# Gated attention and two expert layers on one core: the second unit's first layer, the search marks, the small experts and the last scatters change places

## The chip, the cores and the metric

One core of a Trainium2 chip runs the whole kernel in one launch. The metric is the device time of one execution in microseconds (us), as the median of several runs. A profiled execution of the same program gives the trace; its span is the time from the first to the last instruction on the core. Engines are named as the profile names them: PE (matrix multiplies, with PEld for its weight loads), DVE (VectorE), ACT (ScalarE), POOL (GpSimd) and SP (the queue that issues most DMAs).

## What is computed

```python
def _attn_ref(q, k, v, alpha):                      # 4 x 8 heads, 768 steps, 48 wide
    for t in range(S):
        state = alpha[:, :, t, :, None] * state + np.einsum('bhd,bhe->bhde', k[:, :, t], v[:, :, t])
        y[:, :, t] = np.einsum('bhd,bhde->bhe', q[:, :, t], state)

def _moe_ref(x, w1, w2, w3, w_out):                 # 3072 tokens of 384, hidden 768
    return np.maximum(np.maximum(x @ w1, x @ w2), x @ w3) @ w_out

def _moe2_ref(x, w_gate, w_output_gate, w1, w2):    # 8 experts, hidden 1024
    e_idx = np.argmax(x @ w_gate, axis=1)           # one expert for each token
    for e in range(E):
        mask = e_idx == e
        h = np.maximum(x[mask] @ w1[e], 0.0)
        out[mask] = gate_w[mask, None] * eom[mask, e, None] * (h @ w2[e])
```

## The kernel before, in words

**Stages.** Up to about 456 us of the profile the kernel runs the recurrence and the dense layer, block by block (8 blocks of 384 tokens), and writes the 3072 result rows to a table in DRAM (`x2d`). The rest, which the change touches, is the expert layer. Each product is computed with operands split into a high and a low part, so one product is three matmuls.

**Units.** An expert's tokens are cut into units of up to 256 tokens, two result tiles of 128. A unit is *kind 0* (two tiles, plain), *kind 2* (two tiles and a third of up to 64 tokens) or *kind 3* (one tile). An expert's remaining tokens that fit no unit, up to 64 of them, are a small expert group ("own"). Units 0 and 1 belong to the expert that is largest before the last block is known; their token lists are made early. The lists of all the others are found only when the last block is routed.

**A unit's steps.** `gather` fetches its token rows with one indirect DMA for each tile (POOL queue); `tx` transposes them on PE and splits them (ACT, DVE). `up` is the first layer: 8 groups of 9 matmuls; each group ends in a PSUM bank of the pool `psM`, which has three, and the bank is free when ACT has taken the ReLU (L970) and DVE the low part (L973). `down_tile` is the second layer of one tile: 24 matmuls, then a scaling on ACT (L1017). `send` scatters one tile to the output (POOL queue, L980).

**The list after dense layer and before the loop** is written out by hand (`then(...)`) and every engine runs its instructions in that order: first layer of unit 0, both its tiles (`down_tile(0, 0)`, `down_tile(0, 1)`), first layer of unit 1 in pieces, and among these pieces the search for the other units' tokens. `units_b` computes a slot number for each token; `mark` (L659) then makes, for 24 tiles of 128 tokens and 62 slots, an equality mask on DVE (L669), the mask times the row number on ACT (L670) and the mask times the tile number on DVE (L671). `units_c` multiplies the result with one-hot rows on PE (`lookup`, 24 matmuls, L678) and writes the gather and scatter indices; `units_d`, `units_e` and `units_f` compute the expert, kind and count of each unit on DVE. Then each engine loads these numbers into registers (`values_load`, `load_meta`).

**The loop** is unrolled: `turn(u)` for u from 2, of which turns 2 to 9 always run and later ones are nested, `turn(u + 1)` inside `If(n_all > u + 1)` of turn u. In this run there are 12 units, so turns 2 to 11. A turn starts the next weights, gathers unit u + 2, runs `up(u)`, `tx(u + 1)`, `down(u)` (both tiles, or three, or one, by a branch on the kind), then the small expert i = u - 2 where `n_own > i` (three times here), and scatters unit u with `put(u)`. Where the branch on `n_all` isn't taken, an Else arm holds the last `put(u)`. An arm that issues fewer DMAs than its sibling has a POOL instruction that raises the DMA counters instead (INC_SWDGE_SEM in the profile).

Of the kernel before, what the change touches and what calls it, by code (L numbers as in the profile page):

```python
# [35 lines left out]
NU = 20  # L36
# [13 lines left out]
def kernel(ctx, tc, *args):  # L50
# [9 lines left out]
    def const(shape, name, dt=F32, pool=cst):  # L60
# [10 lines left out]
        pid=const([128, 1], "pid"), tno=const([128, NT], "tno"), meta=const([128, 2 * NU + 1], "meta", I32), kinds=const([128, NU], "kinds", I32), tiny=const([128, NE + 1], "tiny", I32),  # L71
        first=const([128, 2 * NE + 2], "first"), e0=const([128, 1], "e0", I32),
        gidx=const([128, 3 * NU + NE], "gidx", U32), sidx=const([128, 3 * NU + NE], "sidx", U32))
# [20 lines left out]
def _layers(ctx, tc, pool_, wk, K, general, qk, al, a0, v, vT, w123, wout, gates, ew1, ew2, out):  # L94
# [564 lines left out]
    def mark(slot, ids, tiles):  # L659

        w = ids.shape[1]
        def tile(n, name):
            if tiles == NT:
                return bp.tile([128, tiles, n], BF16, tag="x32", name=name)
            return wt([128, tiles, n], name, BF16)

        q, eq = tile(2 * w, "q"), tile(w, "eq")
        sh = [128, tiles, w]
        nc.vector.tensor_tensor(eq, slot.unsqueeze(2).to_broadcast(sh), ids.unsqueeze(1).to_broadcast(sh), ALU.is_equal)  # L669
        nc.scalar.activation(q[:, :, :w], eq, AF.Copy, scale=pid)  # L670
        nc.vector.tensor_tensor(q[:, :, w:], eq, tno[:, :tiles].unsqueeze(2).to_broadcast(sh), ALU.mult)  # L671
        return q

    def lookup(q, units):
        tiles, w = q.shape[1], q.shape[2] // 2
        psi = bank(C["psR"], "R", "psi")
        for g in range(tiles):
            mm(psi[:, :2 * w], C["row"][:, g], q[:, g], start=(g == 0), stop=(g == tiles - 1))  # L678
        it = wt([128, 2 * w], f"it{w}")
        nc.vector.tensor_copy(it, psi[:, :2 * w])  # L680
        a = wt([128, w], f"ia{w}")
        nc.vector.scalar_tensor_tensor(a, it[:, w:], 128.0, it[:, :w], op0=ALU.mult, op1=ALU.add)
        n = 3 if len(units) > NF else 2
        m = len(units) * n

        b = wt([128, w], "le" if w == NS else "ib")
        nc.vector.tensor_scalar(b, it[:, w:], 0.0, 65536.0, op0=ALU.is_equal, op1=ALU.mult)
        parts = [(slice(0, m), True)] + ([(slice(m, w), False)] if w > m else [])
        for cs, three in parts:
            def form(y):  # L690
                return y[:, cs].rearrange("p (u t) -> p u t", t=n) if three else y[:, cs]
            og, os_ = (t[:, :3 * NU].rearrange("p (u t) -> p u t", t=3)[:, units[0]:units[-1] + 1, :n] if three else t[:, 3 * NU:]
                       for t in (gidx, sidx))
            nc.vector.tensor_scalar(og, form(a), -128.0, 0.0, op0=ALU.add, op1=ALU.max)
            nc.vector.scalar_tensor_tensor(os_, form(a), -128.0, form(b), op0=ALU.add, op1=ALU.add)  # L695
# [8 lines left out]
    def first_b():  # L704
# [20 lines left out]
        rtmp["fq"] = mark(fs, ioF, TF)  # L725
# [79 lines left out]
    def units_b():  # L805
# [11 lines left out]
        rtmp["q"] = mark(sl, ioS, NT)  # L817
# [21 lines left out]
    def units_e():  # L839
# [16 lines left out]
        nc.vector.tensor_copy(kinds, kd)  # L856
# [105 lines left out]
    def up_some(u, n, fs):  # L962
        hi, lo = cx[u % 2]
        w1H, w1L = C["w1"]
        for f in fs:
            ps = bank(psM, "M", "psM1")[:, :n]
            for k in range(3):
                for m, (w, x) in enumerate(((w1H, hi), (w1H, lo), (w1L, hi))):
                    mm(ps, w[:, k, f * 128:(f + 1) * 128], x[:, k, :n], start=(k + m == 0), stop=(k + m == 4))  # L969
            nc.scalar.activation(chid(0, f, slice(0, n)), ps, AF.Relu)  # L970
            for a, b, to in ((0, min(n, 256), 384), (256, n, 320)):
                if a < b:
                    nc.vector.scalar_tensor_tensor(C["h"][f // 4][:, f % 4, to:to + b - a], ps[:, a:b], 0.0,  # L973
                                                   chid(0, f, slice(a, b)).bitcast(F32), op0=ALU.max, op1=ALU.subtract)
# [8 lines left out]
    def put(u):  # L983
        def some(*ts):
            for t in ts:
                send(C["y"][t], WIDTH[t], 3 * u + t)
# [32 lines left out]
    def down(u):  # L1019
        down_tile(u, 0)  # L1020
        by_kind(u, {2: lambda: [down_tile(u, t) for t in (1, 2)], 3: lambda: nothing("H")}, lambda: down_tile(u, 1))
# [243 lines left out]

    def put2(u):
# [29 lines left out]
    then(down_tile, 1, 1, low)  # L1296
# [21 lines left out]
    tx(NF)  # L1318
    n_all = nc.values_load(meta[0:1, 2 * NU:2 * NU + 1])
# [5 lines left out]
    load_meta(NF + 1)  # L1325
    K["bad"] = nc.values_load(flags[0:1, 0:1])
# [12 lines left out]
    def turn(u):  # L1339
# [4 lines left out]
        if u + 2 < NU:  # L1344
            load_meta(u + 2)
            gather(u + 2)
# [11 lines left out]
        down(u)  # L1358
        if i < NE:
# [19 lines left out]
    for u in range(NF, NV):  # L1379
        turn(u)  # L1380

# [49 lines left out]
```

## Time and profile before

| | us |
|---|---|
| median of 3 runs (lowest to highest) | 749.11 (748.75 to 749.77) |
| the profiled execution | 747.03 |
| its span | 745.3 |
| PE busy in the span | 701.1 (94%) |
| DVE, ACT, POOL busy | 400.7, 290.8, 127.3 |
| mean granted TensorE clock | 0.985 of full speed |

A row of the profile names a line of the kernel, the engine and the operation, what is written and read, and how often. In brackets stands how long the engine stood idle before it, and what released it. A name that ends in q (ACTq, POOLq) is the engine's instruction queue, where branches, register loads and waits are handled; these count as no busy time.

### The profile page before, as it was taken

The numbers are of one execution on the slowest core, as the hardware profiler recorded it, in microseconds if no ns is written. First come the engines' busy times: TensorE is split into PE (matmuls) and PEld (weight loads), VectorE is DVE, ScalarE is ACT, GpSimd is POOL, SyncE is SP. The second block draws the span as 40 slices with busy tenths as digits, with TensorE's granted clock in tenths as the row PEclk, the third lists the DMA queues.
The fourth block names the chain that finished last, engine by engine and source line by source line (L and its number), as shares of the span: only waits on it lengthen the run. The fifth ranks groups of instructions, "written<-read, shape, count | busy, mean of one in ns | idle before, by whom it ended". The sixth has DMA issues, their size and how long they took to land. (4 is left out here: it accounts for less than half of the span.)

```text
span 745.3 us, 14127 instructions
## 1 busy us (share of the span) xinstructions
PE 701.1 (94%) x5103; PEld 658.9 (88%) x5103; DVE 400.7 (54%) x943; ACT 290.8 (39%) x760; POOL 127.3 (17%) x138
## 2 busy tenths in 40 slices
PE   8999999999899999999999999799999999999990
PEld 7888999888799999999999998789789799999980
DVE  7868886476977646646233275742314454224650
ACT  4445443544543434434222224323324454224640
POOL 1000000011111211201111131142132144232321
PEclk9999999999999999999999999989999999999996
DMA  9815400641510413200000051025456241136321
GB/s 266 348 41 157 146 1 22 184 136 27 144 41 19 127 50 88 57 22 10 12 23 8 33 209 36 22 68 210 187 203 229 107 142 63 49 101 207 116 93 40
DMA packets 23243, 75.38 MB, mean 101 GB/s; under 512 B 8010, under 2 KB 12196, under 8 KB 20064
## 3 DMA queue, kind: packets, MB, share of 16 engines
q1 hardware_dynamic: 17424, 60.95, 24.9%
q0 software_dynamic: 4560, 12.22, 5.4%
q10 hardware_dynamic: 1152, 0.89, 0.5%
q8 instruction: 55, 0.90, 0.5%
q14 instruction: 52, 0.43, 0.2%
HBM read 101.16 MB, written 9.94 MB: 149 GB/s over the span
## 5 line engine op out<-in xcount | busy, mean ns | idle before, releaser
L969 PE MATMUL psM<-cx,w1H 128*128 128x256 f32 (+1 forms) x576 | 112.2, 293 | 12.2 <-DVE ch L973 6.9
L483 POOL TENSOR_TENSOR hL<-hm,hH 128x384 fp32r<-128x384 f32 x36 | 42.2, 1173 | 397.7 <-ACT hH L478 397.6
L457 PE MATMUL hps<-xH,wH 128*128 128x384 f32 x432 | 104.5, 349 | 1.5 <-ACT xH L368 1.3
L969 PEld LDWEIGHTS psM<-cx,w1H 128*128 128x128 f32 x576 | 91.2, 190 | 16.1 <-DVE ch L973 7.9
L457 PE MATMUL hps<-xH,wL 128*128 128x384 f32 x432 | 99.0, 337 | 1.6 <-DVE wL L426 1.6
L457 PE MATMUL hps<-xL,wH 128*128 128x384 f32 x432 | 99.1, 337 | 0.0
L1006 PE MATMUL psP<-w2H,ch 128*128 128x384 f32 x368 | 96.9, 338 | 0.0
L973 DVE SCALAR_TENSOR_TENSOR ch<-psM,ch 128x256 fp32r<-128x256 f32 (+1 forms) x128 | 43.9, 371 | 85.1 <-ACT ch L970 77.5
L969 PE MATMUL psM<-cx,w1L 128*128 128x256 f32 (+1 forms) x288 | 83.6, 290 | 0.9 <-DVEq L1332 0.9
L457 PEld LDWEIGHTS hps<-xH,wH 128*128 128x128 f32 x432 | 74.5, 189 | 7.4 <-ACT xH L368 2.1
L457 PEld LDWEIGHTS hps<-xH,wL 128*128 128x128 f32 x432 | 77.4, 189 | 2.3 <-DVE wL L426 2.3
L457 PEld LDWEIGHTS hps<-xL,wH 128*128 128x128 f32 x432 | 77.9, 189 | 0.1
L493 PE MATMUL ops<-wo,hH 128*128 128x400 f32 x258 | 68.4, 346 | 0.2
L1006 PEld LDWEIGHTS psP<-w2H,ch 128*128 128x128 f32 x368 | 66.7, 188 | 0.7
L970 ACT ACTIVATE ch<-psM 128x256 fp32r<-128x256 f32 (+1 forms) x96 | 37.9, 401 | 71.2 <-PE psM L969 62.1
L464 DVE TENSOR_TENSOR hm<-hm,hps 128x384 f32<-128x384 f32 x48 | 26.4, 551 | 70.7 <-PE hps L457 65.3
L1006 PE MATMUL psP<-w2L,ch 128*128 128x384 f32 x184 | 61.7, 335 | 0.1
L969 PEld LDWEIGHTS psM<-cx,w1L 128*128 128x128 f32 x288 | 54.7, 190 | 1.1 <-DVEq L1332 1.1
L478 ACT CAST hH<-hm 128x384 fp32r<-128x384 f32 x43 | 22.0, 512 | 81.7 <-DVE hm L467 77.9
L980 POOL DMA_INDIRECT out<-yo,sidx x27 | 28.0, 1036 | 132.1 <-ACTq L1360 31.5
L493 PEld LDWEIGHTS ops<-wo,hH 128*128 128x128 f32 x258 | 47.1, 188 | 1.3 <-ACT hH L478 0.5
L893 POOL DMA_INDIRECT xg<-x2d,gidx x40 | 42.2, 1054 | 25.7 <-DVE sidx L695 13.9
(255 smaller groups left out, 1126.8 us busy)
## 6 DMA issues: line engine op xcount, KB each, us to landing
s1a<-in_ew SPq DMA_DIRECT2D x12, 1536.0 KB
s2a<-in_ew SPq DMA_DIRECT2D x12, 1536.0 KB
s1b<-in_ew SPq DMA_DIRECT2D x8, 1536.0 KB
s2b<-in_ew SPq DMA_DIRECT2D x8, 1536.0 KB
ws<-in_w SPq DMA_DIRECT2D x6, 1152.0 KB
at<-in_al SPq DMA_DIRECT2D x16, 336.9 KB
vt<-in_v SPq DMA_DIRECT2D x8, 576.0 KB
x2d<-xs SPq DMA_DIRECT2D x24, 192.0 KB
```

The lines of the kernel that those rows point to most:

```text
L457: mm(ps, slab(a, f)[:, w, k], b[i][:, k], start=(n == 0), stop=(n == 8))
L464: nc.vector.tensor_max(m, m, ps)
L478: nc.scalar.copy(hH[i, f], m)
L483: (nc.gpsimd if not general and i > 1 else nc.vector).tensor_sub(hL[i, f], hps["m"], hH[i, f].bitcast(F32))
L493: mm(ps[:, :DM + NG], a[i, f][:, ts_], wo[f // 3][:, b, f % 3], start=(f + n == 0), stop=(f + n == 7))
L893: nc.gpsimd.indirect_dma_start(out=x[:p], out_offset=None, in_=x2d[:n, :], in_offset=bass.IndirectOffsetOnAxis(ap=gidx[:p, c:c + 1], axis= ...
L969: mm(ps, w[:, k, f * 128:(f + 1) * 128], x[:, k, :n], start=(k + m == 0), stop=(k + m == 4))
L970: nc.scalar.activation(chid(0, f, slice(0, n)), ps, AF.Relu)
L973: nc.vector.scalar_tensor_tensor(C["h"][f // 4][:, f % 4, to:to + b - a], ps[:, a:b], 0.0, chid(0, f, slice(a, b)).bitcast(F32), op0=ALU.m ...
L980: nc.gpsimd.indirect_dma_start(out=out[:, :], out_offset=bass.IndirectOffsetOnAxis(ap=sidx[:p, c:c + 1], axis=0), in_=y[:p], in_offset=Non ...
L1006: mm(ps[:, :DM], chid(x, f, slice(128 * t, 128 * t + 128)), w[:, f], start=(f + n == 0), stop=(f == NE - 1 and n == 2))
```

## The change

- **Order of the list.** Three of unit 1's eight first-layer groups are issued on PE between `down_tile(0, 0)` and `down_tile(0, 1)`, without their ReLU steps. These follow in a new function, `mark_and_up`, after `units_b`.
- **Marks by halves.** The mask work on 24 tiles becomes two halves of 12. The tile-number product of the first half moves from DVE to POOL. A fourth group and its ReLU steps stand between the halves' steps; groups five and six come after them; groups seven and eight after the gather of unit 2 (`NF`).
- **Unit 1's second tile.** Its first half moved behind `tx(NF)`.
- **Small experts.** `own(i)` moves from behind all tiles of unit u to behind its first tile.
- **Gather of unit u + 2** moves into the block of `tx(u + 1)`, and so under `guard(u + 1)`.
- **Last scatters.** The Else arms are gone. Seven more DVE operations in `units_e` copy the last unit's scatter indices and kind to fixed places; one `put(None)` stands behind the whole nest.

```diff
+        def equal(g):
+            sh = [128, g.stop - g.start, w]
+            nc.vector.tensor_tensor(eq[:, g], slot[:, g]..., ids..., ALU.is_equal)
+        def row_no(g):
+            nc.scalar.activation(q[:, g, :w], eq[:, g], AF.Copy, scale=pid)
+        def tile_no(g, e=nc.vector):
+            e.tensor_tensor(q[:, g, w:], eq[:, g], tno[:, g]..., ALU.mult)
...
+        lm = wt([128, NU], "so")
+        nc.vector.tensor_scalar(lm, ioU, end[:, NE - 1:], -1.0, op0=ALU.subtract, op1=ALU.is_equal)
+        nc.vector.tensor_mul(kd, kd, lm)
+        nc.vector.tensor_reduce(ls[:, 3:], kd, op=ALU.add, axis=AX.X)
+        nc.vector.tensor_tensor(rows, sidx[:, 3 * NF:3 * NU]..., lm[:, NF:]..., ALU.mult)
+        nc.vector.tensor_reduce(ls[:, :3], rows, op=ALU.add, axis=AX.X)
+        nc.vector.tensor_copy(kinds[:, NU:], ls[:, 3:])
+        nc.vector.tensor_copy(sidx[:, 3 * NU + NE:], ls[:, :3])
...
+    def mark_and_up():
+        equal, row_no, tile_no = rtmp["mark"]
+        h = [slice(0, NT // 2), slice(NT // 2, NT)]
+        for f in range(3):
+            cut(rtmp[f], 256, f)
+        equal(h[0])
+        row_no(h[0])
+        tile_no(h[0], nc.gpsimd)
+        equal(h[1])
+        row_no(h[1])
+        up_second([3])
+        cut(rtmp[3], 256, 3)
+        tile_no(h[1])
+        up_some(1, 256, range(4, 6))
...
     then(down_tile, 0, 0)
+    then(up_second, range(3))
     then(onehot, i)
     then(down_tile, 0, 1)
     then(put2, 0)
-    then(up_some, 1, 256, range(2))
     then(units_b)
-    then(up_some, 1, 256, range(2, NE - 2))
+    then(mark_and_up)
     then(units_c)
     then(gather, NF)
-    then(up_some, 1, 256, range(NE - 2, NE))
+    then(up_some, 1, 256, range(6, NE))
...
     then(down_tile, 1, 0)
-    then(down_tile, 1, 1, low)
...
     tx(NF)
+    down_tile(1, 1, low)
     n_all = nc.values_load(meta[0:1, 2 * NU:2 * NU + 1])
...
         if u + 2 < NU:
             load_meta(u + 2)
-            gather(u + 2)
         fresh(u, split2, range(2))
         up(u)
...
             with guard(u + 1) as c:
+                if u + 2 < NU:
+                    gather(u + 2)
                 tx(u + 1, own=i < NE)
                 fresh(u + 1, split1)
...
-        down(u)
+        down_tile(u, 0)
         if i < NE:
             with tc.If(n_own > i) as c:
                 own(i)
...
+        down_rest(u)
         if u + 1 < NV:
             put(u)
         elif more:
-            with tc.If(n_all > u + 1) as c:
+            with tc.If(n_all > u + 1):
                 put(u)
                 turn(u + 1)
-            with c.Else():
-                put(u)
-        else:
-            put(u)
...
     for u in range(NF, NV):
         turn(u)
+    put(None)
```

## Rows read from the trace of the kernel before

**Rows 1.** Waits of PE from 456 us on: total, times, longest
```profile
PE psM L969 <- ACTq L1360: 4.3, 5, 1.1
```

**Rows 2.** Busy time by stretch: PE, PEld, DVE, ACT, POOL, clock, DMA share, GB/s
```profile
475.03:480.50 5.47, 5.47 (x46) 5.26 (x45) 2.92 (x9) 1.35 (x3) 1.01 (x1) 1.00 0.10 36
480.50:485.20 4.70, 0.01 (x1) 0.02 (x1) 4.43 (x8) 2.33 (x4) 0.00 (x0) 0.82 0.00 2
485.20:490.30 5.10, 5.10 (x35) 5.00 (x36) 1.30 (x4) 0.40 (x2) 0.00 (x0) 0.50 0.01 3
501.90:504.20 2.30, 0.52 (x3) 0.32 (x3) 0.00 (x0) 0.58 (x1) 0.62 (x1) 1.00 0.76 185
```

**Rows 3.** Timeline of DVE around the marks: start, duration, what
```profile
473.27 0.55 DVE L641 TENSOR_TENSOR row<-io,rmod 128x384 bf16<-128x384 f32 x1
...
478.17 0.35 DVE L809 TENSOR_TENSOR bt<-oh,q 128x192 bf16<-128x192 bf16 x1
...
481.12 1.71 DVE L669 TENSOR_TENSOR eq<-sl,ioS 128x1488 bf16<-128x1488 f32 x1
482.87 1.71 DVE L671 TENSOR_TENSOR q<-eq,tno 128x1488 bf16<-128x1488 bf16 x1
484.70 1.09 DVE L973 SCALAR_TENSOR_TENSOR ch<-psM,ch 128x256 fp32r<-128x256 f32 x3
```

**Rows 4.** Timeline of ACT in the same stretch
```profile
475.30 0.58 ACT L1017 ACTIVATE yo<-psP,gate 128x384 f32<-128x384 f32 x1 [3.58 <-PE psP L1006]
...
482.87 1.54 ACT L670 ACTIVATE q<-eq,pid 128x1488 bf16<-128x1488 bf16 x1 [5.07 <-DVE eq L669]
484.31 0.91 ACT L970 ACTIVATE ch<-psM 128x256 fp32r<-128x256 f32 x3
```

**Rows 5.** Timeline of PE: after the marks, the lookups, the loop's first layer
```profile
485.19 0.80 PE L969 MATMUL psM<-cx,w1H 128*128 128x256 f32 x2 [4.69 <-DVE ch L973]
...
487.28 2.70 PE L678 MATMUL psi<-q,row 128*128 128x124 bf16 x24
...
504.18 0.39 PE L969 MATMUL psM<-cx,w1L 128*128 128x256 f32 x1 [0.92 <-DVEq L1332]
```

**Rows 6.** Timeline of DVE from the lookups to the loop
```profile
490.02 0.29 DVE L680 COPY it<-psi 128x124 f32<-128x124 f32 x1 [1.60 <-PE psi L678]
...
493.18 0.32 DVE L826 TENSOR_TENSOR le<-end,ioU 128x160 bf16<-128x160 f32 x1
...
497.84 0.26 DVE L926 COPY gate<-xg 128x1 f32<-128x1 f32 x3
...
500.77 0.81 DVE L940 TENSOR_TENSOR cx<-psH,cx 128x384 fp32r<-128x384 f32 x2
```

**Rows 7.** L483, one product of two inputs on POOL and on DVE: ns min/median/max
```profile
L483 POOL TENSOR_TENSOR hL<-hm,hH x36: 995/1016/2295, 160.2 to 448.2; 128x384 fp32r<-128x384 f32 x36
L483 DVE TENSOR_TENSOR hL<-hm,hH x7: 550/552/555, 68.9 to 118.6; 128x384 fp32r<-128x384 f32 x7
```

**Rows 8.** Timelines where one turn ends and the next begins
```profile
627.90 0.39 PE L969 MATMUL psM<-cx,w1H 128*128 128x256 f32 x1 [0.70 <-ACTq L1360]
...
630.16 0.42 DVE L973 SCALAR_TENSOR_TENSOR ch<-psM,ch 128x256 fp32r<-128x256 f32 x1 [7.50 <-ACT ch L970]
...
717.98 0.51 PE L969 MATMUL psM<-cx,w1H 128*128 128x256 f32 x2 [1.10 <-DVE ch L973]
```

**Rows 9.** Timeline of ACT, turn 4: the first tile's scaling
```profile
574.09 1.05 ACT L1017 ACTIVATE yo<-psP,gate 128x384 f32<-128x384 f32 x2 [3.24 <-DMA out<-yo,sidx]
```

**Rows 10.** The end: lines 1369 and 1427 (ns min/median/max), then POOL's timeline
```profile
L1369 PEldq COMPARE_BRANCH  x2: 176/2242/4307, 728.0 to 733.3; - x2
...
L1369 POOLq INC_SWDGE_SEM  x1: 1744/1744/1744, 735.0 to 735.0; - x1
...
L1427 POOLq DRAIN  x3: 50/107/6441, 738.0 to 745.0; - x3
...
734.58 1.02 POOL L980 DMA_INDIRECT out<-yo,sidx  x1 [6.57 <-POOLq L1369]
```

More of the change, by code (lines that the diff above doesn't have):

```diff
@@ L667, in mark @@
         q, eq = tile(2 * w, "q"), tile(w, "eq")
[L668 to L672, printed above, removed]
+        def equal(g):
+            sh = [128, g.stop - g.start, w]
+            nc.vector.tensor_tensor(eq[:, g], slot[:, g].unsqueeze(2).to_broadcast(sh), ids.unsqueeze(1).to_broadcast(sh),
+                                    ALU.is_equal)
+        def row_no(g):
+            nc.scalar.activation(q[:, g, :w], eq[:, g], AF.Copy, scale=pid)
+        def tile_no(g, e=nc.vector):
+            e.tensor_tensor(q[:, g, w:], eq[:, g], tno[:, g].unsqueeze(2).to_broadcast([128, g.stop - g.start, w]), ALU.mult)
+        return q, equal, row_no, tile_no
     def lookup(q, units):
@@ L691, in form @@
                 return y[:, cs].rearrange("p (u t) -> p u t", t=n) if three else y[:, cs]
-            og, os_ = (t[:, :3 * NU].rearrange("p (u t) -> p u t", t=3)[:, units[0]:units[-1] + 1, :n] if three else t[:, 3 * NU:]
+            og, os_ = (t[:, :3 * NU].rearrange("p (u t) -> p u t", t=3)[:, units[0]:units[-1] + 1, :n] if three else t[:, 3 * NU:3 * NU + NE]
                        for t in (gidx, sidx))
@@ L724, in first_b @@
         nc.vector.scalar_tensor_tensor(fs, fs, -64.0, rdiv[:, :TF], op0=ALU.mult, op1=ALU.add)
-        rtmp["fq"] = mark(fs, ioF, TF)
+        rtmp["fq"], *steps = mark(fs, ioF, TF)
+        for f in steps:
+            f(slice(0, TF))
     def first_c():
@@ L816, in units_b @@
         nc.vector.tensor_add(sl, sl, so)
-        rtmp["q"] = mark(sl, ioS, NT)
+        rtmp["q"], *rtmp["mark"] = mark(sl, ioS, NT)
     def units_c():
@@ L960, in halves, with up_one, cut, up_some @@
             mm(ps[64 * g:64 * g + 64, :n], x[g], w[g], start=start, stop=stop, skip_group_check=True)
-    def up_some(u, n, fs):
+    def up_one(u, n, f):
         hi, lo = cx[u % 2]
         w1H, w1L = C["w1"]
-        for f in fs:
[L966 to L974, printed above, removed]
+        ps = bank(psM, "M", "psM1")[:, :n]
+        for k in range(3):
+            for m, (w, x) in enumerate(((w1H, hi), (w1H, lo), (w1L, hi))):
+                mm(ps, w[:, k, f * 128:(f + 1) * 128], x[:, k, :n], start=(k + m == 0), stop=(k + m == 4))
+        return ps
+    def cut(ps, n, f):
+        nc.scalar.activation(chid(0, f, slice(0, n)), ps, AF.Relu)
+        for a, b, to in ((0, min(n, 256), 384), (256, n, 320)):
+            if a < b:
+                nc.vector.scalar_tensor_tensor(C["h"][f // 4][:, f % 4, to:to + b - a], ps[:, a:b], 0.0,
+                                               chid(0, f, slice(a, b)).bitcast(F32), op0=ALU.max, op1=ALU.subtract)
+    def up_some(u, n, fs):
+        for f in fs:
+            cut(up_one(u, n, f), n, f)
     def up(u):
@@ L985, in some @@
             for t in ts:
-                send(C["y"][t], WIDTH[t], 3 * u + t)
+                send(C["y"][t], WIDTH[t], 3 * NU + NE + t if u is None else 3 * u + t)
         by_kind(u, {2: lambda: some(1, 2), 3: lambda: None}, lambda: some(1))
@@ L1017, in down_tile, with down_rest @@
         nc.scalar.activation(C["y"][t], ps[:, :DM], AF.Copy, scale=gate[u % 2][:, t:t + 1])
-    def down(u):
-        down_tile(u, 0)
-        by_kind(u, {2: lambda: [down_tile(u, t) for t in (1, 2)], 3: lambda: nothing("H")}, lambda: down_tile(u, 1))
+    def down_rest(u):
+        by_kind(u, {2: lambda: [down_tile(u, t) for t in (1, 2)], 3: lambda: nothing("R")}, lambda: down_tile(u, 1))
     def own(i):
@@ L1264, in then, with up_second @@
         rest.append((f, a))
+    def up_second(fs):
+        for f in fs:
+            rtmp[f] = up_one(1, 256, f)
+    def mark_and_up():
[12 more added lines that the diff above has]
+        up_some(1, 256, range(4, 6))
     def put2(u):
@@ L1325, in _layers @@
     load_meta(NF + 1)
+    kind[None] = nc.values_load(kinds[0:1, NU:], engines=(ET.Pool,))
     K["bad"] = nc.values_load(flags[0:1, 0:1])
```

10 lines of the change are left out of this document (7 added, 3 removed).

## The prediction

> **What bounds the kernel now.** The table of engines comes first: PE is busy for 701.1 of 745.3 us, so only the places where PE stands still, or runs at half clock, can be won. The waits of PE from 456 us on show most of them: in five turn ends the first layer waited for ACT's queue, 4.3 us in all, none over 1.1 us [rows 1]. The larger place stands ahead of the loop. At 485.19 PE comes back after 4.69 us [rows 5]. The timelines of DVE and ACT say why: all three banks of psM are filled, and the steps that empty them stand behind the marks; DVE runs its two whole marks from 481.12 to about 484.6 and cuts from 484.70 [rows 3], ACT has the row-number product at 482.87 ahead of its ReLUs [rows 4]. The idle time is paid twice: in the next 5.1 us, all busy, the granted clock is 0.50 (1.2 GHz) [rows 2], and half of that, 2.55 us, would not have been spent at 2.4 GHz. Then PE waits in the loop's first layer for DVE's queue, 0.92 us before 504.18 [rows 5]. The third place is the end: POOL stands idle for 6.57 us before the last send at 734.58, and its drain of 6.44 us ends the span [rows 10].
>
> **The start: -5.0 us (bounds -6.5 and -1.5).** I follow the new order step by step. 45 matmuls took about 5.3 us at full clock [rows 2], so a group of nine costs 1.06 and three groups 3.18. They now stand ahead of the second result tile of unit 0, whose scaling on ACT began at 475.30 [rows 4]; it moves to 475.30 + 3.18 = 478.48. Only behind it come the ReLUs, at about 479.0, and the three cuts, which took 1.09 from 484.70 [rows 3], from 479.4 to 480.5. PE needs the first cut before its fourth group; that came 0.49 after the cuts' start (485.19 - 484.70), hence at 479.9. PE is done with the tile at 478.2, so **a wait of 1.7 us** takes the place of the 4.69.
>
> The slot numbers (478.17 to 481.12 on DVE [rows 3], 2.95 us) now follow the row at 473.27 directly and end near 476.8, under PE's three groups and tile. Each half mark has 744 elements. DVE took 0.55 for 384 and 1.71 for 1488 [rows 3], 1.05 ns an element between them, so a half costs 0.93: equality masks at 480.5 to 481.4 and 481.4 to 482.35. ACT's row-number halves at half of 1.54 [rows 4] end near 483.2, and the fourth cut and the second tile-number half on DVE near 484.9. **The half moved to POOL** has no row of its own; the nearest is a product of two inputs of 384 elements on POOL, 1016 ns in the median and 2295 at worst [rows 7]. For 744 that makes 1.97 or 4.45 us, ending at 483.4 or 485.9. I take the first; it is then ahead of DVE's half and costs nothing, and the worst costs about 1.0. That it is cheaper than hidden is excluded, since DVE's half ends later.
>
> The Trainium skill speaks against this step: "GPSIMD Engine Reference", section "Engine selection", gives elementwise work on two inputs to VectorE and calls GpSimd about half as fast. The rows agree (1016 against 552 ns [rows 7]). Twice 0.93 would be 1.86 by it, an estimate, and the sum the same as by the rows; by its advice, both halves on DVE, the start would give -4.1.
>
> The 24 lookups took 2.70 at half clock [rows 5], so 1.35 at full clock. Their second half follows 484.9 and the copy of the result stands at 486.0 instead of 490.02 [rows 6]: **-4.0 so far**. The last two groups of unit 1 cost 2.1 at 2.4 GHz, so the counting on DVE moves from 493.18 [rows 6] to about 488.9. From there to the gate copies at 497.84 [rows 6] stood 4.66 us; seven new small DVE operations at 0.2 each (between the 0.26 for three one-element copies and the 0.29 of a 124-element copy [rows 6]; bounds 0.1 and 0.3) add 1.4, so the gates are copied near 495.0, and the last split of unit 2's tokens, which on DVE follows the gates and takes 0.81, comes near 495.8 where it was 500.77 [rows 6]. From that split to PE's next product in the loop lay 3.41 us (500.77 to 504.18 [rows 5, 6]), register loads and a branch in DVE's queue; so PE's turn begins at 499.2 instead of 504.18, **-5.0**. POOL's one new register load (the last unit's kind) is not on this way. The first half of unit 1's second tile, moved behind the transposes, gives PE work while ACT and DVE split; PE itself would be ready near 497.5, so DVE decides, and that move gains nothing more. The gather of unit 2 is issued from 487 instead of 491, so it is not late.
>
> The clock: before, it fell after 4.69 us with almost no PE work, and stayed at 1.00 through 501.90 to 504.20, where PE was busy for 0.52 of 2.30 us [rows 2]. The new waits are of about 1.7 us, so I keep 2.4 GHz. The bounds: -6.5 if the wait is nearly filled (1.5 less), -1.5 if the clock falls once (2.55) and POOL is at its worst row (1.0).
>
> **Small experts between the tiles: -1.7 us (bounds -2.6 and +1.5).** Where a small expert stands at a unit's end, the next unit's first layer waits for the branch in ACT's queue behind it: 0.70 before 627.90 [rows 8]. Moved, this wait goes, and the next thing that is late is the first cut. In that turn it ran from 630.16 for 0.42 [rows 8], to 630.58, while PE had stopped at 627.20; PE's three groups take 3.18, so 0.2 of each wait stays (0 by the lower bound). The five waits of 4.3 us [rows 1] are three of this kind and two of about 1.1 behind kind 2 units, where weight casts stand ahead of the ReLU; of the three 0.5 each is won, -1.5; of the two 0.25 each, -0.5, since at 717.98 no small expert stands and 1.10 is waited all the same [rows 8]. Three small experts now stand ahead of the last tile, and their copies on ACT stand behind the scaling of the unit's first tile. That scaling waited 3.24 us for an earlier scatter in turn 4 [rows 9]; behind it now queue the small expert's steps and PE's second tile. Most often PE has a tile's worth of work in hand: +0.3 in all, or +3.24 if one such wait shows fully. -1.5 - 0.5 + 0.3 = -1.7.
>
> **The tail: 0 (bounds -3.4 and +3.5).** Without Else arms the path not taken must still raise the DMA counters: 1.74 us for one such instruction [rows 10]. At the end of this run it now stands ahead of the last send, not behind it. The gathers of a unit that does not exist, now under the guard, fall away, but their counters must be raised too. So POOL does one to three of these, 1.7 to 5.2, in the stretch in which it idled or gathered, and one fewer after the send. The branch of 4.31 us on PE's queue at line 1369 [rows 10] shows what a jump over the nested code costs; it stays, since the jump does. I put the send between 732.9 and 739.8, around 734.58, and the drain's start 1.74 nearer to it: -3.4 to +3.5 at the span's end, and take 0. Else, the gathers keep their place among POOL's instructions, so queues move nothing.
>
> **Sum:** -5.0 - 1.7 + 0 = -6.7. The span goes from 745.3 to 738.6, the profiled execution, 1.73 above the span, from 747.03 to 740.3. The median of the runs stood 2.1 above that execution: **742.4 us**.
>
> **Rivals.**
> - *The clock falls at the new wait.* The wait of 1.7 and the slower lookups keep PE idle twice within a few us. Then up to 5.1 us run at 0.50 again, 2.55 more [rows 2]: 744.9. For: 4.69 us were enough; against: 2.30 us with 0.52 of work were not. The Trainium skill names this pattern in "TensorE: Matmul & The Clock Gate", section "HAM oscillation — how this bites in real kernels": a wait on another engine throttles the array, and the work behind it starts cold. The stretch at 0.50 behind the 4.69 us agrees.
> - *The turn ends give nothing.* The small expert's steps wait for a scaling that waits for a scatter, 3.24 [rows 9], while the waits are won: +1.5 instead of -1.7, so 742.4 + 3.2 = 745.6; with all five waits kept as well, 747.3.
> - *The change does not arrive.* PE is early at the loop, but the tail takes it back at its upper bound, +3.5, and the clock its 2.55: 742.4 + 6.0 = 748.4, within 0.2% of the time before.
> - *Slower: POOL's half mark becomes the bound.* Its tile numbers are broadcast and bf16, which no POOL row has. If it takes X us, the lookups come X - 3.5 late, and all of unit 2 with them. At X = 10 that is 6.5, PE is idle over 4.69 and the clock falls (2.55): 742.4 + 9.0 = 751.4. It crosses 749.11 near X = 7.7, 10.3 ns an element against 2.65 in the median and 6.0 at worst [rows 7].
>
> **How the numbers follow.** Forecast 0.58; clock 0.13; turn ends 0.09; not arriving 0.11; slower 0.09. The low end takes the start at -6.5, the turn ends at -2.6 and half of the tail's gain: 742.4 - 1.5 - 0.9 - 1.7 = 738.3. The high end covers the clock and the turn ends' worst, 747.3. What can be told from no change is 0.2%, 1.5 us. Faster: the first three, 0.80; same 0.11; slower 0.09.
>
> **What would show it.** Right: PE's wait near 479 of 1 to 2 us at a granted clock of 1.00; the copy of the lookups near 486; the loop's first matmul at 498 to 500; no wait on line 1360's queue over 0.3; the drain's start within 3.5 of the last unit's end as before. Wrong: a granted clock of 0.50 anywhere from 479 to 490; a POOL product over 4.5 us; a first layer waiting for DVE's cut by more than 0.5 in the turns; more than one counter instruction between the last matmul and the last send.

## The result and the profile after

| | before | changed |
|---|---|---|
| median of four runs each on the chip of the first comparison, us | 748.93 | 738.21 |
| ratio (95% interval) | | 0.9861 (0.9841 to 0.9881) |
| median on a second chip (11 and 6 runs), us | 746.31 | 737.73 |
| ratio (95% interval) | | 0.9878 (0.9860 to 0.9896) |
| the profiled execution, us | 747.03 | 738.47 |
| its span, us | 745.3 | 736.8 |

The change is faster by 8 to 11 us, where 6.7 was forecast. By the spans it is 8.5.

To see where, every trace of this study is cut at two marks: the first product of unit 0's first layer, ahead of all that the change touches, and the end of unit 10's last product on PE, when one unit is left. The table is worked out from the traces of all the kernels, those of the experiments too. A is the time from the first mark to the second, B from there to the span's end, A + B their sum; "loop" is the part of A up to the loop's first product with the low part of the weights (504.18 in [rows 5]).

| kernel | first mark at | loop | A | B | A + B |
|---|---|---|---|---|---|
| before | 456.8 | 47.4 | 257.1 | 31.5 | 288.6 |
| before, again | 460.1 | 47.5 | 258.2 | 30.9 | 289.2 |
| changed | 456.9 | 42.5 | 249.0 | 30.9 | 279.8 |
| changed, again | 456.1 | 41.9 | 249.0 | 31.0 | 279.9 |
| start_as_before | 458.3 | 47.7 | 254.0 | 30.6 | 284.6 |
| own_behind | 456.2 | 42.5 | 252.9 | 29.0 | 281.9 |
| tail_as_before | 460.1 | 42.5 | 248.6 | 29.9 | 278.5 |
| gather_as_before | 457.1 | 41.8 | 248.5 | 34.0 | 282.5 |
| last_longer | 457.2 | 41.8 | 248.9 | 30.0 | 278.9 |
| marks_whole | 457.0 | 42.5 | 248.6 | 31.2 | 279.8 |
| tile_no_dve | 455.9 | 43.6 | 249.9 | 30.6 | 280.5 |
| low_as_before | 457.5 | 43.1 | 249.6 | 30.4 | 280.0 |
| cuts_early | 456.7 | 39.5 | 246.3 | 30.9 | 277.1 |
| cuts_early_else | 458.6 | 44.5 | 253.5 | 29.9 | 283.4 |

The first mark wanders by up to 4.2 us between executions, for one and the same program too (456.8 and 460.1); A of the changed kernel repeats within 0.1. So A + B is what compares kernels by one profile each. Of the 8.7 us between the first two profiles, 8.1 lie in A and 0.6 in B; of the 9.3 between the second two, all lie in A. B scatters by 2.2 us among kernels with one and the same tail (29.0 to 31.2), so small differences are read from A.

The waits of PE from 456 us on, of the changed kernel (in total, times, longest), beside [rows 1], and below them the line for DVE's cuts of the kernel before:

```profile
PE psM L990 <- DVE ch L997: 5.6, 6, 1.5
PE psP L1034 <- issue: 1.1, 1, 1.1
PE psM L990 <- DVEq L1380: 0.4, 1, 0.4
```

```profile
PE psM L969 <- DVE ch L973: 6.9, 5, 4.7
```

The line for ACT's queue, 4.3 us in [rows 1], is gone. What is left waits for DVE's cuts, none over 1.5. These waits grew where the change did not aim at them: 5.6 without the 1.46 below makes 4.1, where 6.9 without the 4.69 made 2.2. The timeline of PE, the places with a wait ahead of the loop:

```profile
480.03 0.51 PE L990 MATMUL psM<-cx,w1H 128*128 128x256 f32 x2 [1.46 <-DVE ch L997]
...
483.67 0.82 PE L686 MATMUL psi<-q,row 128*128 128x124 bf16 x12 [0.29 <-POOL q L678]
484.90 0.84 PE L686 MATMUL psi<-q,row 128*128 128x124 bf16 x12 [0.41 <-DVE q L678]
...
496.38 0.41 PE L1034 MATMUL psP<-w2H,ch 128*128 128x384 f32 x1 [1.05 <-issue]
...
499.38 0.39 PE L990 MATMUL psM<-cx,w1L 128*128 128x256 f32 x1 [0.41 <-DVEq L1380]
```

One wait of 4.69 [rows 5] has become three, of 1.46, 0.29 and 0.41. Nearer to the loop the wait for DVE's queue fell from 0.92 to 0.41, and 1.05 between the halves of the moved tile is new, while PE's queue loads registers. The clock stays up through them; windows as in [rows 2], of the same stretch and of the way to the loop:

```profile
478.60:485.50 6.90, 4.77 (x50) 4.50 (x51) 4.70 (x9) 3.97 (x9) 3.05 (x2) 1.00 0.09 32
485.50:499.40 13.90, 12.43 (x83) 11.62 (x80) 8.69 (x47) 3.10 (x7) 7.66 (x8) 1.00 0.28 76
```

The granted clock is 1.00 (2.4 GHz) where it was 0.50 for 5.1 us. DVE, POOL and ACT on that way:

```profile
479.55 1.09 DVE L997 SCALAR_TENSOR_TENSOR ch<-psM,ch 128x256 fp32r<-128x256 f32 x3 [2.70 <-ACT ch L994]
480.55 1.77 DVE L671 TENSOR_TENSOR eq<-sl,ioS 128x744 bf16<-128x744 f32 x2
...
485.77 0.29 DVE L688 COPY it<-psi 128x124 f32<-128x124 f32 x1 [0.27 <-PE psi L686]
...
488.70 0.32 DVE L836 TENSOR_TENSOR le<-end,ioU 128x160 bf16<-128x160 f32 x1
...
492.40 0.23 DVE L869 TENSOR_SCALAR so<-ioU,end 128x20 f32<-128x20 f32 x1
...
493.47 0.17 DVE L878 CAST sidx<-fc 128x3 uint32<-128x3 f32 x1
...
494.66 0.26 DVE L948 COPY gate<-xg 128x1 f32<-128x1 f32 x3
495.89 0.82 DVE L962 TENSOR_TENSOR cx<-psH,cx 128x384 fp32r<-128x384 f32 x2 [0.51 <-ACT cx L961]
```

```profile
481.57 2.05 POOL L678 TENSOR_TENSOR q<-eq,tno 128x744 bf16<-128x744 bf16 x1 [1.03 <-DVE eq L671]
```

```profile
495.38 0.70 ACT L961 CAST cx<-psH 128x384 fp32r<-128x384 f32 x2 [0.97 <-PE psP L1034]
```

The forecast had the cuts at 479.4, the masks at 480.5, the copy of the lookups at 486.0, the counting at 488.9, the gates at 495.0 and the last split at 495.8. Each came within 0.4.

### The profile page after: what moved, and what is told of

Read it like the earlier page. It is cut to its first block, busy times and chain, and to the rows that moved or that the text cites. A ratio compares the mean times of both kernels' runs of the same rounds, so it can differ in the third digit from the quotient of the medians.

```text
span 736.8 us, 14113 instructions
## 1 busy us (share of the span) xinstructions
PE 699.1 (95%) x5103; PEld 656.9 (89%) x5103; DVE 399.7 (54%) x951; ACT 290.4 (39%) x761; POOL 124.5 (17%) x136
## 5 line engine op out<-in xcount | busy, mean ns | idle before, releaser
L990 PE MATMUL psM<-cx,w1H 128*128 128x256 f32 (+1 forms) x576 | 110.3, 290 | 5.6 <-DVE ch L997 5.6
L483 POOL TENSOR_TENSOR hL<-hm,hH 128x384 fp32r<-128x384 f32 x36 | 42.2, 1172 | 397.9 <-ACT hH L478 397.9
L1034 PE MATMUL psP<-w2H,ch 128*128 128x384 f32 x368 | 99.3, 341 | 1.1 <-issue 1.1
L493 PE MATMUL ops<-wo,hL 128*128 128x400 f32 x129 | 44.5, 345 | 0.5 <-POOL hL L483 0.5
```

Of the source, the lines that this page charges most:

```text
L483: (nc.gpsimd if not general and i > 1 else nc.vector).tensor_sub(hL[i, f], hps["m"], hH[i, f].bitcast(F32))
L493: mm(ps[:, :DM + NG], a[i, f][:, ts_], wo[f // 3][:, b, f % 3], start=(f + n == 0), stop=(f + n == 7))
L1034: mm(ps[:, :DM], chid(x, f, slice(128 * t, 128 * t + 128)), w[:, f], start=(f + n == 0), stop=(f == NE - 1 and n == 2))
```

## The experiments

Two theories run through them. The forecast's: start, turn ends and tail are three separate sums, -5.0, -1.7 and 0. Its rival, from the traces: the turns give about 3, and the tail is a chain of its own on POOL. The runs were taken on three chips on which the median of before was 747.58, 746.31 and 747.35, so the kernels are compared by A and B first. The kernels gather_as_before, last_longer, marks_whole, tile_no_dve and low_as_before ran once each, the others five to twelve times.

**The kernel before, again.** The median of before lies 2.1 above its profiled execution; this run asks why.

> The kernel before, run again, to learn where its runs differ: the profiled execution took 747.03 us, the median 749.11. Theory 1: the difference lies in the stall ahead of the loop, and so in how long the TensorE clock stays at 0.50 behind it: runs near 749 have a mean granted clock below 0.985 by about 2 x 2.1/745 = 0.005, and a profile of such a run shows the loop's first full product later than 504.2. Theory 2: the difference lies elsewhere (the first 456 us, transfers): the mean clock stays at 0.985 and the loop begins at 504.2 after a first part that is as long or longer by up to 2 us.

Median 748.22 over 12 runs, from 745.78 to 751.01; the profiled one took 751.01. Windows of its trace, and of own_behind for the same first 100 us:

```profile
0.00:100.00 100.00, 94.64 (x758) 88.63 (x759) 77.40 (x106) 44.42 (x119) 3.08 (x21) 0.97 0.55 179
...
505.00:515.00 10.00, 8.37 (x55) 7.85 (x55) 1.84 (x6) 2.51 (x6) 2.03 (x2) 0.83 0.89 336
```

```profile
0.00:100.00 100.00, 95.13 (x775) 89.09 (x775) 79.91 (x110) 45.21 (x121) 3.06 (x21) 1.00 0.56 179
```

The number ahead of the last two is the clock: in the first 100 us it was 0.97 in one execution and 1.00 in another, of code that the change doesn't touch. The stall at the marks was 4.69 in both profiles of before. Theory 1 falls for the most part: the scatter comes from stretches at 0.50 in the first stage, and once, 1.2 us, from one at the loop's beginning (0.83 above).

Each of these early stretches, in all the profiles, begins 0.2 to 2.2 us after PE has waited for 1.3 to 2.0 us at one of three places, near 11, 60 and 153 us. The same wait is not followed by one in every execution. Behind a wait of 1.33 that ended at 151.31, in the first profile of before, and of 1.32 that ended at 151.58, in the second profile of the change:

```profile
152.40:155.80 3.40, 3.40 (x12) 3.30 (x12) 2.83 (x12) 0.67 (x4) 0.00 (x0) 0.50 0.50 97
```

```profile
152.70:156.10 3.40, 3.40 (x20) 3.17 (x20) 2.80 (x12) 0.67 (x4) 0.00 (x0) 1.00 0.53 85
```

**Small experts behind all tiles again.**

```diff
-        down_tile(u, 0)
-        ... own(i) ...
-        down_rest(u)
+        down_tile(u, 0)
+        down_rest(u)
+        ... own(i) ...
```

> The changed kernel with the small expert behind all tiles of a unit again, all else as changed. The forecast's price of this move is -1.7 us, so 738.2 + 1.7 = 739.9. The traces, loop start to last product, give the turns -3.0 (224.1 to 221.1 us), so 741.2 if all of that is this move. Rival: the waits come back but cost nothing at the end because POOL's sends end the run: 738.2 to 738.6. In the profile five waits of 0.7 to 1.1 us at turn ends on ACT's queue should be back.

Median 739.83; A + B is 281.9, 2.0 more than the change. In A the move is worth 3.9, and the wait for ACT's queue is back:

```profile
PE psM L990 <- ACTq L1410: 4.5, 5, 1.3
```

But B is 1.9 shorter, 29.0: the last scatter of unit 10 went out 8.5 us after that unit's end instead of 9.2 to 9.5, and the drain took 6.88 instead of 7.83. So half of what the turns win was not seen at the end; whether the move or the scatter of B is the cause, one profile can't tell. The median lies 1.6 and 2.1 above the two medians of the change, which were taken on other chips.

**Else arms again.**

```diff
-            with tc.If(n_all > u + 1):
+            with tc.If(n_all > u + 1) as c:
                 put(u)
                 turn(u + 1)
+            with c.Else():
+                put(u)
-    put(None)
```

with the seven operations and the load of the last kind left out.

> The changed kernel with the Else arms and their scatters again, and so without the seven DVE operations, the register load of the last kind and the last scatters behind all branches. The forecast priced the tail at 0 and the seven operations at 1.4 us on the way to the loop: 738.2 - 1.4 = 736.8 by it. By the trace of the changed kernel the tail from the last product to the end became 0.7 shorter, and PE at the loop's start waits only 0.4 for DVE's queue, so the operations cost no more than 0.4: 738.2 + 0.7 - 0.4 = 738.5. Rival: the Else arm's counter instruction behind the last send costs its whole 1.74: 739.5 to 740.

Median 739.80 with a first mark at 460.1 in its profile; A + B is 278.5, 1.3 less than the change. "Loop" is 42.5 with the operations and 42.5 without: they cost nothing that can be seen there. In both profiles another thing, ACT's late copies of the transposes, held DVE's split (see the account of the start below). B is 29.9 with Else arms; with the tail as changed it lies between 29.0 and 31.2 in nine other profiles. The last scatters behind all branches gain nothing that can be seen. In this pair and in the last one below they cost 1.0 and 0.9, which is less than that scatter.

**Old order of the list, whole marks.**

> The changed kernel with the old order of the list and whole marks, small experts, gather and last scatters as changed. Forecast: the start is worth 5.0 us, 743.2, of which 2.55 is a stretch at 0.50 granted clock behind a wait of about 4.7 us at the marks; that stretch should be back. If the scatter of the old kernel's runs (2.1 us between its profiled run and its median) belongs to this stall, the median is 745.3 and its runs scatter by 2 us again, against 1.3 of the changed kernel. With the seven DVE operations still there, up to 1.4 more.

Median 743.86 and A + B 284.6, 4.8 more than the change; A is 5.0 more, and "loop" 5.2 to 5.8. The wait and the stretch behind it are back, on PE's timeline and in the windows:

```profile
486.65 0.79 PE L990 MATMUL psM<-cx,w1H 128*128 128x256 f32 x2 [4.69 <-DVE ch L997]
```

```profile
486.70:491.80 5.10, 5.10 (x36) 5.01 (x37) 1.27 (x4) 0.38 (x1) 0.00 (x0) 0.50 0.01 3
```

So the start is worth what the forecast said; the eight runs lie at 0.9928 of before (0.9903 to 0.9954), the change at 0.9861.

**The changed kernel again**, for the kernels on the second chip.

> The changed kernel again, on the chip of these runs, so that the kernels with one part undone have their counterpart. From unit 0's first product to the end the trace gave 279.8 us (before: 288.6 and 289.2 in two profiles); what comes ahead of that product differed by up to 3.9 us between profiles of one and the same program. Expected: 279.8 within 0.6 from that product on, 8.7 less than before; median 738 to 739 beside 747.6 to 749 for the kernel before.

279.9, as expected; median 737.73 beside 746.31.

**A longer last unit.**

```diff
         down_rest(u)
+        if u == 11:
+            for _ in range(2):
+                ps = bank(C["psH"], "H", "psN")
+                for f in range(8):
+                    mm(ps[:, :DM], C["h"][0][:, 0, 0:128], C["w2"][0][:, f], ...)
```

> The changed kernel with 16 more products of 384 columns (0.173 us each, 2.8 us in all, read by nobody) on PE behind the last unit's tiles. Theory: the end of the run hangs on POOL, which goes from unit 10's scatters, one after the other, through counter instructions and a code fetch to the last send; the last unit's 14.6 us on PE are covered by it. Then the end comes 30.9 us after unit 10's last product as before this edit (within 0.6). Rival: PE's end sets the tail, +2.8. By the forecast, which priced the tail from the last send and took PE's end as its beginning, also +2.8.

PE works 2.7 us longer and the end doesn't move: B is 30.0 (30.9 and 31.0 without). PE of this kernel, then the sends on POOL of this kernel:

```profile
720.40 3.02 PE L1420 MATMUL psN<-w2H,ch 128*128 128x384 f32 x16
```

```profile
707.55 1.34 POOL L1008 DMA_INDIRECT out<-yo,sidx  x1 [11.87 <-ACT ylo L1023]
711.29 0.93 POOL L1008 DMA_INDIRECT out<-yo,sidx  x1 [2.41 <-DVE ch L997]
715.70 1.00 POOL L1008 DMA_INDIRECT out<-yo,sidx  x1 [3.47 <-ACT ch L994]
728.05 0.98 POOL L1008 DMA_INDIRECT out<-yo,sidx  x1 [11.36 <-issue]
```

and the same four of the changed kernel:

```profile
707.31 1.33 POOL L1008 DMA_INDIRECT out<-yo,sidx  x1 [11.82 <-ACT ylo L1023]
711.05 0.93 POOL L1008 DMA_INDIRECT out<-yo,sidx  x1 [2.41 <-DVE ch L997]
715.38 0.99 POOL L1008 DMA_INDIRECT out<-yo,sidx  x1 [3.40 <-ACT ch L994]
727.76 0.98 POOL L1008 DMA_INDIRECT out<-yo,sidx  x1 [11.38 <-issue]
```

Its counter instruction at the skipped turn, and its drain (ns):

```profile
L1419 POOLq INC_SWDGE_SEM  x1: 1641/1641/1641, 721.0 to 721.0; - x1
...
L1474 POOLq DRAIN  x3: 50/113/7832, 728.1 to 736.5; - x3
```

The first send comes 1.43 us after unit 10's end, the next ones 3.7 and 4.3 to 4.4 apart, the last 12.4 after the third, in both. The last unit's 14.6 us on PE are covered by this chain.

**Gather ahead of the first layer, unguarded.**

```diff
             load_meta(u + 2)
+            gather(u + 2)
...
             with guard(u + 1) as c:
-                if u + 2 < NU:
-                    gather(u + 2)
```

> The changed kernel with the gather of unit u + 2 ahead of the unit's first layer and outside the guard again. The forecast gave this move nothing. In the trace it takes three gathers of a unit that does not exist (about 1.3 us each) from POOL behind unit 10's scatters and puts one counter instruction of 1.65 in their place. If POOL sets the end, the end comes 2.0 to 2.5 us later after unit 10's last product (33.0 instead of 30.9). Rival: the gathers go out while POOL waits for the scatters anyway: 0 or 0.5.

B is 34.0, 3.1 more than the change, and A 0.4 less. POOL's timeline has the three gathers of a unit that doesn't exist inside the chain:

```profile
715.29 1.00 POOL L1008 DMA_INDIRECT out<-yo,sidx  x1 [3.56 <-ACT ch L994]
716.60 1.05 POOL L915 DMA_INDIRECT xg<-x2d,gidx  x1 [0.30 <-issue]
717.95 1.06 POOL L915 DMA_INDIRECT xg<-x2d,gidx  x1 [0.30 <-DVE w2L L646]
719.31 0.95 POOL L915 DMA_INDIRECT xg<-x2d,gidx  x1 [0.30 <-issue]
731.34 1.02 POOL L1008 DMA_INDIRECT out<-yo,sidx  x1 [11.07 <-issue]
```

From the third send to the last it is 16.0 us here and 12.4 in the change. The run's time, 741.37 in one execution beside a median of 737.73, agrees. With Else arms the same guard is worth less: B is 29.9 with it (tail_as_before) and 31.5 and 30.9 without (before), so 3.1 is its price on this tail only.

**Whole marks in the new order.**

```diff
-        equal(h[0]); row_no(h[0]); tile_no(h[0], nc.gpsimd)
-        equal(h[1]); row_no(h[1])
+        equal(slice(0, NT)); row_no(slice(0, NT)); tile_no(slice(0, NT))
         up_second([3])
         cut(rtmp[3], 256, 3)
-        tile_no(h[1])
```

> The changed order of the list, with the marks as whole operations on DVE and ACT (1.71, 1.54 and 1.71 us) in the place of the halves, nothing on POOL. By the forecast the halves let the row numbers and the first lookups begin early; by the trace the whole masks would end at 480.55 + 1.71 + 1.71 = 483.97 and the lookups need 1.65 from there, 485.6, where the changed kernel's ended at 485.73. So the halves are worth nothing and the loop's first full product comes 41.8 to 42.5 us after unit 0's first product, as in two profiles of the change. Rival: they are worth 0.9 or more because the fourth group's ReLU stands behind the whole row-number product: 42.8 to 43.4.

"Loop" is 42.5, A + B 279.8: the halves are worth nothing. PE waits once for the lookups, 0.68, where the halves wait 0.29 and 0.41:

```profile
484.12 1.50 PE L686 MATMUL psi<-q,row 128*128 128x124 bf16 x24 [0.68 <-DVE q L678]
```

**The first half's tile numbers on DVE.**

```diff
-        tile_no(h[0], nc.gpsimd)
+        tile_no(h[0])
```

> The changed kernel with the first half's tile numbers on DVE instead of POOL. The forecast (and the rule it weighed) said DVE's chain grows by 0.93 and the loop begins 0.9 later, 42.7 to 43.4 us after unit 0's first product. By the trace DVE stood idle for 1.25 us before 483.57, waiting for ACT's ReLU, so the half fits there: 41.8 to 42.5, and the lookups' wait of 0.29 for POOL goes.

"Loop" 43.6 and A 249.9, 0.9 more than the change: the forecast's price, not the 0 that I expected here. DVE and PE of this kernel:

```profile
480.47 0.93 DVE L678 TENSOR_TENSOR q<-eq,tno 128x744 bf16<-128x744 bf16 x1
481.32 0.93 DVE L671 TENSOR_TENSOR eq<-sl,ioS 128x744 bf16<-128x744 f32 x1
```

```profile
484.82 0.83 PE L686 MATMUL psi<-q,row 128*128 128x124 bf16 x12 [1.81 <-DVE q L678]
```

The product stands ahead of the second mask; the mask, ACT's row numbers, the fourth ReLU and cut and the second product all move by it, so the idle time ahead of the cut does not take it up. The whole marks do without POOL and lose nothing: in their trace the product follows the mask on DVE at once, at 482.36 behind 480.63 and 1.70.

**First half of unit 1's second tile ahead of the transposes again.**

```diff
+    then(down_tile, 1, 1, low)
...
     tx(NF)
-    down_tile(1, 1, low)
```

> The changed kernel with the first half of unit 1's second tile ahead of unit 2's transposes again. The forecast said that the move gains nothing because DVE's register loads set the loop's start: 41.8 to 42.5 us after unit 0's first product. In the trace of the change ACT's cast of the second transpose waited until 495.38, when the moved half ended at 495.33; ahead of the transposes it would end at 494.2 and the cast follow the transposes near 495.5, the same. Rival: the move covers the split with work of PE, and without it PE waits 1 us or more: 43.4.

"Loop" 43.1, A 249.6: the move is worth 0.6, between the two expectations. The reason that I gave here for ACT's late cast, the moved half tile, is not it: in the second profile of the change the casts were on time with the half tile at the same place.

**The cuts ahead of the scaling.** The wait of 1.46 is left over; these steps of ACT and DVE stand behind the scaling of a tile that they don't need.

```diff
-    then(down_tile, 0, 1)
-    then(put2, 0)
+    then(down_tile, 0, 1, range(NE), False)
     then(units_b)
+    then(lambda: [cut(rtmp[f], 256, f) for f in range(3)])
+    then(scale_tile, 0, 1)
     then(mark_and_up)
+    then(put2, 0)
```

> The changed kernel with the ReLUs and cuts of unit 1's first three groups issued ahead of the scaling of unit 0's second tile (and behind the slot numbers on DVE), and the scatters of unit 0 behind the marks. Theory: the wait of 1.46 us ahead of the fourth group is there because these steps stand behind that scaling on ACT; DVE is free at 476.85, so the cuts run from about 477 instead of 479.55, PE goes on at 478.6 without a wait, and with the waits of 0.29 and 0.41 at the lookups 2.2 us are won; the loop's first full product comes 40.3 to 40.6 us after unit 0's first product instead of 42.46, the median is 2 us lower. Rival: DVE's and ACT's register loads ahead of the loop set its start, whatever PE does before: under 0.5 us is won. Second rival: the ReLU must wait for the tile's last product that reads the same buffer: 0.5 to 1 us won.

Median 735.25 (733.85 to 736.30) beside 737.73 (737.00 to 737.84) of the change on the same chip; ratio to before 0.9846 (0.9824 to 0.9868). A + B 277.1, 2.7 less than the change; "loop" is 39.5, 0.8 below the best that I expected. The cuts run at 476.49 instead of 479.55 and the waits ahead of the fourth group and the lookups are gone from the list; what is late next is a gathered tile:

```profile
476.49 1.08 DVE L997 SCALAR_TENSOR_TENSOR ch<-psM,ch 128x256 fp32r<-128x256 f32 x3
```

```profile
PE psH L951 <- DMA xg<-x2d,gidx: 0.9, 1, 0.9
```

It is the fastest kernel of this study.

**That, with the Else arms.**

> The kernel with the cuts ahead of the scaling, and with the Else arms and their scatters as in the kernel before (no last scatters behind all branches, no seven operations). If the parts add, the end comes 29.9 us after unit 10's last product instead of 30.9, and the loop's first full product 39.4 us after unit 0's first product as with the cuts alone: 277.1 - 1.0 = 276.1 from that product on, a median of 734.2 where the cuts alone had 735.25 and the change 737.73. Rival: the tail's 1.0 was the scatter's and the drain's own variation between runs (0.5 to 1.2 us in the profiles so far): 735.2.

Median 741.97 beside 747.35 of before: slower than the change in all six runs (740.41 to 744.03). B is 29.9 as expected, but "loop" is 44.5 instead of 39.5. PE stood for 4.13 us at the loop; PE's timeline, then ACT's:

```profile
501.99 0.50 PE L978 MATMUL psM<-cx,w1H 128*128 128x256 f32 x2 [4.13 <-ACTq L1370]
```

```profile
496.83 0.48 ACT L949 CAST cx<-psT 128x384 fp32r<-128x384 f32 x1 [4.33 <-issue]
499.06 0.70 ACT L949 CAST cx<-psH 128x384 fp32r<-128x384 f32 x2 [1.75 <-PE psP L1022]
```

ACT began to copy the first transposes about 5 us after PE had written them, and the profile names no releaser ("issue"). The granted clock then was 0.52 over the 7.0 us from 502.20. The same copies were late by 0.8 and 1.0 in one profile of the change, on time in the other of the same program, and on time in cuts_early. Why, stays open, and so it is not shown that the Else arms cost this.

## Why the prediction was right, and where its sizes were off

**The start, -5.0: right in sum, and in nearly every step.** "Loop" went from 47.4 to 42.5, -5.0 (-5.6 in the second pair). The new wait was 1.46 for 1.7, POOL's half 2.05 for 1.97, the clock stayed at 1.00. What was wrong is which list decides. The forecast had PE ready near 497.5, so that DVE sets the start, the seven operations cost 1.4 and the moved half tile gains nothing. PE came to the loop at 498.57, as it stood for 1.05 between the tile's halves, which the sum left out, and putting the half tile back cost 0.6. The seven operations took about 1.2 (492.40 to 493.64), but no cost of theirs was seen. In the first profile of the change the split behind them waited 0.51 for ACT's copy of the transposes, which came late, at 495.38. In the second this copy was on time:

```profile
492.13 0.71 ACT L961 CAST cx<-psH 128x384 fp32r<-128x384 f32 x2
```

There DVE's split followed its own list at 494.52, and PE went into the loop at 497.75 without a wait: PE's own list decided, and "loop" is 41.9. By the forecast's own 3.41 from the split to PE's product, DVE's list would have let PE begin at 497.93, nearly the same time. The three paths, over PE, over DVE's list and over ACT's late copies, end within 0.6 us of each other, so that the sum came out at -5.0 is in part luck.

The halves were costed as a gain in the sum; whole marks in the new order do as well. What counts is the order: three groups ahead of the tile, and their cuts ahead of the marks; the moved half tile is 0.6 of it.

On POOL's half, the rows first: 2.05 us for what took DVE 0.93 in the experiment, 2.2 times as long; yet on DVE it cost 0.9 more. With whole marks, both products on DVE cost nothing (A 248.6), so POOL only makes good what the halving costs. The Trainium skill ("GPSIMD Engine Reference", section "Engine selection") gives such products to VectorE and calls GpSimd about half as fast. The price agrees; its advice cost 0.9 with the halves and nothing with whole marks.

**The turn ends, -1.7: right in sign, too small.** From the loop's start to unit 10's end it became 206.5 from 209.6, -3.1; own_behind puts the move alone at 3.9 within A. The term that failed is the price of what is late next at a plain turn end. The forecast took the first cut's end of the kernel before, 630.58 [rows 8], from PE's end at 627.20, though PE had itself begun 0.70 late there. DVE and ACT of the changed kernel at the same place, where PE begins at 621.73:

```profile
624.30 0.76 DVE L997 SCALAR_TENSOR_TENSOR ch<-psM,ch 128x256 fp32r<-128x256 f32 x2 [7.04 <-ACT ch L994]
```

```profile
623.82 0.67 ACT L994 ACTIVATE ch<-psM 128x256 fp32r<-128x256 f32 x2 [1.16 <-ACTq L1380]
```

The first cut is done near 624.7, 3.0 after PE's beginning, and three groups take 3.18: the 0.70 is won whole, three times. That is 0.6 of the missing 1.4. The small experts' own turns were given +0.3; turns 2 to 4 together became 0.4 us shorter than before, and 1.1 shorter than in own_behind. At a unit with a third tile nothing was won in the first case, as the wait moved three groups on:

```profile
606.56 0.51 PE L990 MATMUL psM<-cx,w1H 128*128 128x256 f32 x2 [1.18 <-DVE ch L997]
```

In the second case 0.73 was left of 1.08; the forecast had 0.25 for each. What remains, 0.4, isn't placed. Over the whole run, with B, the move is worth 2.0 by A + B, near the 1.7. That nearness is luck: it is 3.9 in A against 1.9 the other way in B.

**The tail, 0: near (-0.6, and 0.0 in the second pair), for a wrong reason.** The forecast counted from PE's end. last_longer shows that the end hangs on POOL from unit 10's sends on. On that chain the guard around the gather is worth 3.1, which the forecast let cancel against the counter instructions. What the last scatters behind all branches cost or gain there lies within the 2.2 us by which B differs among kernels with one and the same tail. That part of B varies with the scatters (3.3 to 4.5 us between the second and the third) and with the drain (6.9 to 8.4); what sets these is open.

**The sum.** By the profiles -8.7 for a forecast of -6.7; the missing 2 are the turns' 1.4 and the tail's 0.6. (In the second pair it is -9.3: -5.6 in the start, -3.6 in the turns, where 1.2 is the low clock at before's loop, and nothing in the tail.) The median moved by 10.7, to 738.2, just below the range's low end of 738.3, because the forecast carried the 2.1 between profile and median of before over to the change. In the profile of before that took 751.01, most of such a difference lay in stretches at 0.50 in the first 456 us; the changed kernel's profile happened to lie at its median. That does not settle it: the runs of before lie between 744.87 and 752.05, the ten of the change between 737.00 and 739.02, with the same first stage. Why before scatters more stays open. On the second chip the medians differ by 8.6.

**The rivals.** The clock didn't fall: it was 1.00 through 1.46, 0.29 and 0.41 us of waiting within 6.9 us, and no lower in any of the nine profiles with a wait of 1.46 or 1.47 there. In start_as_before, behind 4.69 us, it fell to 0.50. The Trainium skill warns of such a loss in "TensorE: Matmul & The Clock Gate", section "HAM oscillation — how this bites in real kernels"; start_as_before agrees. But that the waits here were shorter does not explain it, since waits of 1.3 to 2.0 us were followed by 0.50 in the first stage of some executions, so this rival was nearer than the forecast's argument for 2.4 GHz allows. POOL's half mark took 2.05, a quarter of the price at which the change would have lost. "The turn ends give nothing" didn't come: the turns won 3.1. Its price of +1.5 isn't the sum of its terms either, which is -1.5 - 0.5 + 3.24 = +1.24. "The change does not arrive" didn't come, as the tail took nothing back.

**The signs.** Those of "right" came: 1.46 at a clock of 1.00, the copy of the lookups at 485.77, the loop's first matmul at 498.57, no wait for ACT's queue at the turn ends, the drain's start 7.6 behind the last unit's end (9.8 before). Two of "wrong" came too. First layers in the turns waited 1.18, 0.73 and 1.10 for DVE's cut: that is the mis-sized term of the turn ends (the 1.10 stood there before). And three counter instructions, at 721.05, 723.13 and 724.81, ran between the last matmul at 720.47 and the last send: that is POOL's chain, which the forecast did not follow.

## What to carry to other kernels

Ask of a stall which steps stand between the buffer and its release only by the order of the list; the new order of the list was worth 5 us, most of it three groups and their cuts, and cutting the work behind them in halves was worth nothing. Look for the chain that ends the run on the queue engine too: a run whose last sends, counters and drain take 31 us hides the last unit's whole arithmetic, and work for units that do not exist costs there what it seems to cost nowhere else. And compare kernels from a mark ahead of the change: here one program's executions differed by up to 5 us, its stage behind the mark by about 0.1 unless the clock fell there. Take a second profile, too: one program had ACT's copies late in one and on time in the other.

## What was not expected of the hardware

- In its first 200 us, which the change doesn't touch, an execution had none to three stretches at 0.50 granted clock (one and three in two profiles of before, one and none in two of the change), each behind a PE wait of 1.3 to 2.0 us that in other executions left the clock at 1.00. The first mark follows: 455.9 to 456.2 with none, 460.1 with three.
- Raising a DMA counter on POOL takes 0.59 us early in the loop and 1.6 to 1.7 at its end; three to five of them and the drain (6.2 to 8.4 us) make up 36 to 48% of the tail.
- A scatter to the output waited, by the program's semaphores, for the landing of the one before it: sends of one unit lie 3.3 to 4.5 us apart though each takes about 1 us on POOL. In gather_as_before the first landed at 710.0 and the next went out at 710.8; that landed at 714.4, and the third went out at 715.3.
- ACT's copy of PE's transposes started up to 5 us after they were written (cuts_early_else), without a releaser in the profile, and in one program it was on time in one execution and late in another (492.13 and 495.38).
